# Agent attention with two feed-forward layers: an earlier query load, a second order for the last steps, shared PSUM tiles in the first block, and GpSimd rounding in 23 steps

## The chip, the core and the metric

The kernel runs on one core of a Trainium2 chip. The metric is device time in microseconds (us). The kernel before takes 1104.78 us (median of 3 runs, 1104.61 to 1104.95).

## The reference

For 12480 tokens of width 128 and 49 agents, with a softmax over the last axis of scaled products:

```python
agent_v = softmax(scale * agents @ k.T) @ v
x       = softmax(scale * q @ agents.T) @ agent_v
h  = x @ moe_w_in                                  # 128 -> 2048
g  = where(h >= 1, h, where(h <= -1, 0, (h + 1)**2 / 4))
y  = g @ moe_w_out                                 # 2048 -> 128
h2 = y @ moe2_w_in
out = (s * relu(h2)**2 + b) @ moe2_w_out
```

## The kernel before, in words

Products are made from operands split into a rounded high part and a low rest (type fp32r): high·high, high·low and low·high are added in PSUM.

**Prologue** (`agents_values`, up to about 68 us): key scores, softmax over tokens, `agent_v`, decoding of the weights, and the product of `agent_v` with the first layer's weights, left in `awh` and `awl` by `weights_high` (L500) and `weights_low` (L504).

**Blocks and steps.** The tokens stand in 25 blocks: the first 256 wide, then 23 of 512, the last 448. A block has 8 steps in each layer (`JP`), and a step makes two chunks of 128 of the 2048 hidden features, so there are 200 steps (`NS`). A narrow step's elementwise tile is 128x512 (two chunks of 256 tokens), a wide one's 128x1024.

**One step of layer 1** is a chain over the engines: `H` on TensorE (L602, or the pair L632 and L638 from block 2 on), `R` on ScalarE (`relu`, L651), `S` on ScalarE (`square`, L657), `M` on VectorE (`cap`, L661, reads PSUM and SBUF), `g` the rounding to the high part (`hi`: L670 on ScalarE or L672 on VectorE), `L` on VectorE (`lo`, L677: two SBUF inputs, the low part), `O` on TensorE (L716, summed over the block's 8 steps in PSUM tile `y`). Layer 2 has the same letters in small (`h r s l o`; in the steady lists `t` is the square, `G` and `C` the rounding on ScalarE or VectorE), with no cap, and its sum lies in PSUM tile `o`. `Y` and `y` take the sum of layer 1 out as high and low part (L735, L738); `Z` takes the result out (L742) and issues its DMA. Layer 2 runs `D` = 11 steps behind layer 1.

**Who rounds.** `PAT1` = "10011010001001" says it for the first 14 steps of layer 1 (1 is ScalarE: steps 0, 3, 4, 6, 10, 13); all other steps of layer 1 round on VectorE. Layer 2 follows `PAT2`, three quarters on ScalarE, and its last 11 steps round on VectorE. GpSimd does nothing after the constants at the start.

**Queries.** `load_q(t)` (L160) issues block t's queries on the SP queue into one of two buffers. `q_scores` (L169) makes 4 products with the agents, and ten small operations on ScalarE and VectorE (`z` in the ramp's order: L176, L186 to L199) make the softmax. `q_transpose` (L212) turns it to `pt`; from block 2 on, SP also issues two DMAs `pt<-pt` and four `px<-pt` (L226, L228), whose rows the second half of the pair step (L638) reads.

**PSUM.** Tag `h` has three tiles of two banks, one tile per H or h, per `q_scores` and per `q_transpose`. Tags `y` and `o` have one bank each.

**Order.** Each engine works its queue in program order, and the program's order is written out. After the prologue, `fill_rows` (L607) issues eight DMAs on SP that copy `awh` and `awl` into other layouts. Then `ramp` (L749) follows the string `RAMP`, from H of step 0 to step 13. Then `steady` (L767) takes the steps two at a time: for each pair `n0` it adds the tokens of `PAIR` to a list per engine, and a loop emits from the lists while dependencies hold. In `PAIR`, layer 1's step is n0 or n0+1, the layer 2 step of `h` and `r` is m = n - 11, `t`, `G`, `C` and `l` are of step m-1, `O` is n-2 and `o` is m-2. The same lists serve the last pairs (n0 = 200 to 214), where no H is left.

Of the kernel before, what the change touches and what calls it, by code (L numbers as in the profile page):

```python
# [18 lines left out]
def kernel(  # L19
# [17 lines left out]
    nc = tc.nc  # L37
    P = 128
# [8 lines left out]
    XN = 2 * X1  # L47
    XL = NA - XN

    GR, XB, UB, WB, KV = 4, 3, 4, 2, 7  # L50
    WARM, CD = 10, 1
    PAT1, PAT2, TL = "10011010001001", "11011101", 11

# [22 lines left out]
        "v11 v12 D1 q1"  # L76
    )
    RAMP = (
# [5 lines left out]
    )  # L84
    WORD = "A0 A2 A1 B0 B1 C0 C1 D0 D1".split()
    PIECE = {"A0": (0, 512), "A2": (512, 512)}
# [2 lines left out]
        "PE": "H0 h0 O0 o0 q0 O1 p1 p0 h1 q1 o1".split(),  # L89
        "ACT": "t0 P0 Y0 R0 R1 Q0 S0 S1 G0 r0 P1 Y1 t1 r1 Q1 G1".split(),  # L90
        "DVE": "L0 y0 C0 C1 Z1 F0 M0 M1 l0 Z0 c0 y1 c1 L1 l1 F1".split(),
    }
    QS, QT, DX = 7, 5, 1
    MASK_H = 0x7FFFFE00
# [64 lines left out]
        q_t[t] = qp.tile([P, TB], F32, tag="q", name=f"q{t}")  # L159
        nc.sync.dma_start(out=q_t[t][:, :w], in_=qT[:, t0:t0 + w])  # L160

    def q_scores(t):
        if t >= NB:
            return []
        qt = q_t.pop(t)
        sc = ps_h(f"qs{t}")
        scv = sc[:, 0, 0:4 * NA].rearrange("p (c a) -> p c a", a=NA)
        for i, c0 in enumerate(subs(t)):
            nc.tensor.matmul(out=scv[:, i, :], lhsT=qt[:, c0:c0 + P], rhs=aT, start=True, stop=True)  # L169
        e = small.tile([P, 4, NA], F32, tag="qe", name=f"qe{t}")  # L170
        mx = small.tile([P, 4], F32, tag="qm", name=f"qm{t}")
        sm = small.tile([P, 4], F32, tag="qsm", name=f"qsm{t}")
        pt = ptok[t % NPT]
        parts = [(P, 0, len(subs(t)))]
        ops = [
            lambda n=n, a=a, b=b: nc.scalar.activation(out=e[:n, a:b, :], in_=scv[:n, a:b, :], func=ACTF.Copy)  # L176
            for n, a, b in parts
        ]
        qev.extend(ops)
        ops = []  # L180
        for n, a, b in parts:
            ev, mv, sv = e[:n, a:b, :], mx[:n, a:b], sm[:n, a:b]
            wide = [n, b - a, NA]
            ph, pl = pt[:n, a:b, 0:NA], pt[:n, a:b, LO:LO + NA]
            ops += [
                lambda ev=ev, mv=mv: nc.vector.tensor_reduce(out=mv, in_=ev, op=ALU.max, axis=AX.X),  # L186
                lambda ev=ev, mv=mv, wide=wide: nc.vector.tensor_tensor(
                    out=ev, in0=ev, in1=mv.unsqueeze(2).to_broadcast(wide), op=ALU.subtract
                ),
                lambda ev=ev: nc.scalar.activation(out=ev, in_=ev, func=ACTF.Exp, scale=scale),  # L190
                lambda: None,
                lambda ev=ev, sv=sv: nc.vector.tensor_reduce(out=sv, in_=ev, op=ALU.add, axis=AX.X),
                lambda sv=sv: nc.vector.tensor_scalar_add(sv, sv, 1e-9),
                lambda sv=sv: nc.vector.reciprocal(out=sv, in_=sv),
                lambda ev=ev, sv=sv, wide=wide: nc.vector.tensor_tensor(
                    out=ev, in0=ev, in1=sv.unsqueeze(2).to_broadcast(wide), op=ALU.mult
                ),
                lambda ev=ev, ph=ph: nc.vector.tensor_copy(out=ph, in_=ev),
                lambda ev=ev, ph=ph, pl=pl: nc.vector.tensor_tensor(  # L199
                    out=pl, in0=ev, in1=ph.bitcast(F32), op=ALU.subtract  # L200
                ),
            ]
        return ops

    def q_transpose(t):
        if t >= NB:
            return
        fill(len(fillers))
        w = blocks[t][1]
        tp = ps_h(f"tp{t}")[:, 0, :]  # L210
        for i, c0 in enumerate(subs(t)):
            nc.tensor.matmul(  # L212
                out=tp[:, c0:c0 + P], lhsT=ptok[t % NPT][:, i, :], rhs=ident_r,
                start=True, stop=True,
            )
        pt = pt_t[t] = ptp.tile([P, TB], F32R, tag="pt", name=f"pt{t}")
        if t >= QB:
            px = px_t[t] = late.tile([P, TB], F32R, tag="px", name=f"px{t}", bufs=2)

        def spread():  # L220
            nc.scalar.activation(out=pt[:, :w], in_=tp[:, :w], func=ACTF.Copy)
            if t < QB:
                return
            src = pt.bitcast(F32)
            for i, r in enumerate((NA, LO + NA)):
                nc.sync.dma_start(out=src[r:r + X1, :w], in_=src[i * X1:(i + 1) * X1, :w])  # L226
            for g in range(P // RG):
                nc.sync.dma_start(out=px.bitcast(F32)[g * RG:g * RG + XL, :w], in_=src[XN:NA, :w])  # L228

        qev.append(spread)  # L230
# [353 lines left out]
    D1, D2 = 2, 2  # L584
    D = JP + D1 + DX
    hp, gx, gh, gl = {}, {}, {}, {}
    y_ps, y_hl, o_ps = {}, {}, {}

    def H(layer, n):
        t, j = divmod(n, JP)  # L590
        w = blocks[t][1]
        h = ps_h(f"h{layer}_{n}")
        for i in range(2):
            sl = slice((2 * j + i) * P, (2 * j + i + 1) * P)
            if layer == 1:
                rhs = pt_t[t][:, :w]
                ops = [(awh, rhs), (awl, rhs)]
            else:
                yh, yl = y_hl[t]
                ops = [(wi2h, yh[:, :w]), (wi2h, yl[:, :w]), (wi2l, yh[:, :w])]  # L600
            for m, (a, r) in enumerate(ops):
                nc.tensor.matmul(  # L602
                    out=h[:, i, :w], lhsT=a[:, sl], rhs=r, start=(m == 0), stop=(m == len(ops) - 1)
                )
        hp[layer, n] = h
# [54 lines left out]
        x, h = gv(gx, 1, n), gv(hp, 1, n)  # L660
        nc.vector.scalar_tensor_tensor(out=x, in0=h, scalar=1.0, in1=x, op0=ALU.max, op1=ALU.min)  # L661

    def hi(layer, n, on_act):
        kind = GH(layer, n)
        if (kind == "1") != on_act:
            return
        gh[layer, n] = ring("gh", layer, n, F32R, GR)
        x, a = gv(gx, layer, n), gv(gh, layer, n)
        if on_act:
            nc.scalar.activation(out=a, in_=x, func=ACTF.Copy)  # L670
        else:
            nc.vector.tensor_copy(out=a, in_=x)  # L672

    def lo(layer, n):
        gl[layer, n] = ring("gl", layer, n, F32R, GR)
# [7 lines left out]

    def GH(layer, n):
        if layer == 1:
            return PAT1[n] if n < len(PAT1) else "0"
        return PAT2[n % len(PAT2)] if n < NS - TL else "0"

    def last_step(first):
# [59 lines left out]
    def ramp():  # L749
        steps = {}  # L750

        def first_q(k):
            ops = q_scores(k)
            steps[k] = [q_evac, *ops[:3], *ops[4:]]

        does = {
            "H": lambda n: H(1, n), "R": lambda n: relu(1, n), "S": lambda n: square(1, n), "M": cap,
            "g": lambda n: hi(1, n, GH(1, n) == "1"), "L": lambda n: lo(1, n), "O": lambda n: O(1, n),
            "h": lambda n: H(2, n), "r": lambda n: relu(2, n), "s": lambda n: square(2, n),
            "G": lambda n: hi(2, n, GH(2, n) == "1"), "l": lambda n: lo(2, n), "o": lambda n: O(2, n),  # L760
            "Y": lambda: evac(1, "h"), "y": lambda: evac(1, "l"),
            "u": load_q, "q": first_q, "p": q_transpose, "P": lambda n: q_evac(), "z": lambda k, i: steps[k][i](),
        }
        for token in RAMP.split():
            does[token[0]](*[int(x) for x in token[1:].split(".") if x])

    def steady():  # L767

        lists = {e: [] for e in PAIR}

        def first(n):
            t, j = divmod(n, JP)
# [15 lines left out]
            fillers.extend(later.pop(0))  # L788

        for n0 in range(NR, NS + D + D2 + 2, 2):  # L790
            for e, tokens in PAIR.items():
                for token in tokens:
                    c, n = token[0], n0 + int(token[1])
                    m, j, t = n - D, n % JP, n // JP
# [5 lines left out]
                        return [slots[-4]] if len(slots) > 3 else []  # L800

                    def add(key, deps, fn, *args):
                        lists[e].append((key, deps, fn, args))

                    if c == "H" and a and n == n0:
                        add(("H", n), slot(("M", n)) + slot(("M", n + 1)), first, n)
# [20 lines left out]
                    elif c == "M" and a:  # L827
                        add(("M", n), [("S", n)], cap, n)
                    elif c == "c" and a:
                        add(("c", n), [("M", n), ("O", n - GR)], hi, 1, n, False)  # L830
                    elif c == "L" and n - 1 < NS:
                        add(("L", n - 1), [("c", n - 1), ("O", n - 1 - GR)], lo, 1, n - 1)
                    elif c == "r" and 0 <= m < NS - 1:
# [3 lines left out]
                    elif c == "t" and 0 <= m - 1 < NS - 1:  # L837
                        add(("t", m - 1), [("r", m - 1)], square, 2, m - 1)
                    elif c in "GC" and 0 <= m - 1 < NS - 1 and (c == "G") == (GH(2, m - 1) == "1"):
                        add(("g", m - 1), [("t", m - 1), ("o", m - 1 - GR)], hi, 2, m - 1, c == "G")  # L840
                    elif c == "l" and 0 <= m - 1 < NS - 1:
                        add(("l", m - 1), [("g", m - 1), ("o", m - 1 - GR)], lo, 2, m - 1)
                    elif c == "l" and m - 1 == NS - 1:
# [20 lines left out]
    with tc.manual_schedule():  # L864
        prologue()
        late = ctx.enter_context(tc.tile_pool(name="late", bufs=1))
        fill_rows()
        ramp()
        fillers.append(lambda: nc.vector.tensor_scalar_mul(bcol, bcol, b_sb[:, 0:1]))
# [36 lines left out]
```

## Time and profile before

| | us |
|---|---|
| runs, median of 3 | 1104.78 |
| the profiled execution | 1106.68 |
| its span, first to last instruction | 1104.9 |
| busy in the span: TensorE, ScalarE, VectorE | 1072.0, 969.9, 964.8 |
| busy GpSimd, all in the first 2 us | 0.8 |

The profiled execution is 1.90 us (0.17%) above the median, and 1.78 us of it lie outside the span. Busy times are shares of one execution; TensorE's are modelled, since matmuls overlap. An entry like `[5.12 <-DMA q<-in_qT]` behind an instruction says that its engine was idle that long before it and what ended the idle time. `x2` means that the row holds two consecutive instructions.

### The profile page before, as it was taken

To read this page: it belongs to the slowest core of one execution; us is meant where nothing else is said; L and a number is where in the kernel's file an instruction comes from. 1 tells how busy PE (TensorE), PEld (TensorE's weight loads), DVE (VectorE), ACT (ScalarE), POOL (GpSimd) and SP (SyncE) were. 2 spreads that over 40 slices of the span, in tenths; PEclk is the share of its full clock that TensorE was granted. 3 is DMA by queue.
4 is the path that set the end of the run, shared out by engine and by line. 5 is a ranking of instruction groups with operands and counts; after the bars stand their busy time and mean duration, and the time that the engine had idled before them with its cause. 6 is when DMAs were issued, how large, how long until landed. Compare 5 with 4: busy or idle time off the path is not lost.

```text
span 1104.9 us, 13492 instructions
## 1 busy us (share of the span) xinstructions
PE 1072.0 (97%) x5050; PEld 823.4 (75%) x5050; DVE 964.8 (87%) x1194; ACT 969.9 (88%) x1132; POOL 0.8 (0%) x7
## 2 busy tenths in 40 slices
PE   6887999999999999999999999999999999999997
PEld 2676777777777777777777777777777777777776
DVE  8887889889889889889889889889889889889875
ACT  6876899889889889889889989989989989989974
POOL 0000000000000000000000000000000000000000
PEclk9898999999999999999999999999999999999999
DMA  9920000000000000000000000000000000000000
GB/s 351 394 79 23 19 23 24 4 28 24 4 28 25 3 28 25 3 27 26 3 27 26 3 27 26 2 27 27 1 28 27 1 27 27 1 18 18 1 10 18
DMA packets 19973, 41.01 MB, mean 37 GB/s; under 512 B 2638, under 2 KB 7976, under 8 KB 19268
## 3 DMA queue, kind: packets, MB, share of 16 engines
q1 hardware_dynamic: 19908, 40.15, 10.6%
q8 instruction: 40, 0.66, 0.3%
q14 instruction: 25, 0.20, 0.1%
HBM read 27.58 MB, written 6.39 MB: 31 GB/s over the span
## 4 chain that ended last, share of the span: by engine, by line
PE 89%; DVE 5%; ACT 2%; DMA 1%; SPq 1%; issue 1%; DVEq 0%
PE h L602 26%; PE o L716 24%; PE y L716 23%; PE h L632 7%; PE h L638 4%; PE qs L169 2%; DVE gl L677 1%; DMA k<-in_kT 1%; DVE x L661 1%; PE tp L212 1%; PE av L457 1%; ACT x L657 1%; SPq L616 1%; DVE gh L672 1%; DVE mxs L414 1%
## 5 line engine op out<-in xcount | busy, mean ns | idle before, releaser
L677 DVE TENSOR_TENSOR gl<-x,gh 128x1024 fp32r<-128x1024 f32 (+2 forms) x399 | 469.4, 1193 | 20.0 <-ACT gh L670 19.8
L657 ACT ACTIVATE x<-x 128x1024 f32<-128x1024 f32 (+2 forms) x399 | 404.4, 1043 | 1.9
L661 DVE SCALAR_TENSOR_TENSOR x<-h,x 128x1024 f32<-128x1024 f32 (+2 forms) x200 | 230.5, 1192 | 77.0 <-ACT x L657 76.4
L653 ACT ACTIVATE x<-h 128x1024 f32<-128x1024 f32 (+2 forms) x199 | 201.3, 1012 | 59.6 <-PE h L602 59.6
L651 ACT ACTIVATE x<-h 128x1024 f32<-128x1024 f32 (+2 forms) x200 | 190.0, 1005 | 2.9 <-DVE gl L677 1.0
L672 DVE CAST gh<-x 128x1024 fp32r<-128x1024 f32 (+2 forms) x251 | 164.0, 678 | 15.4 <-ACT x L657 15.2
L602 PE MATMUL h<-yh,wi2h 128*128 128x512 f32 (+2 forms) x400 | 166.7, 417 | 0.9 <-DVE x L661 0.9
L716 PE MATMUL o<-gl,wo2h 128*128 128x512 f32 (+2 forms) x400 | 157.9, 395 | 5.2 <-DVE gl L677 5.2
L716 PE MATMUL o<-gh,wo2h 128*128 128x512 f32 (+2 forms) x400 | 157.7, 394 | 1.9 <-DVE osb L742 1.8
L716 PE MATMUL y<-gl,wo1h 128*128 128x512 f32 (+2 forms) x400 | 156.6, 391 | 1.3 <-DVE gl L677 1.3
L716 PE MATMUL y<-gh,wo1h 128*128 128x512 f32 (+2 forms) x400 | 156.2, 391 | 0.1
L716 PE MATMUL y<-gh,wo1l 128*128 128x512 f32 (+2 forms) x400 | 156.2, 390 | 0.0
L716 PE MATMUL o<-gh,wo2l 128*128 128x512 f32 (+2 forms) x400 | 155.6, 389 | 0.0
L602 PE MATMUL h<-yh,wi2l 128*128 128x512 f32 (+2 forms) x400 | 155.5, 389 | 0.0
L602 PE MATMUL h<-yl,wi2h 128*128 128x512 f32 (+2 forms) x400 | 155.4, 389 | 0.0
L670 ACT ACTIVATE gh<-x 128x1024 fp32r<-128x1024 f32 (+1 forms) x148 | 152.2, 1030 | 0.9 <-DVE x L661 0.8
L602 PEld LDWEIGHTS h<-yh,wi2h 128*128 128x128 f32 x400 | 75.0, 187 | 36.7 <-issue 17.0
L632 PE MATMUL h<-pt,awm 128*128 128x512 f32 (+1 forms) x368 | 99.2, 391 | 0.0
L716 PEld LDWEIGHTS o<-gl,wo2h 128*128 128x128 f32 x400 | 75.0, 188 | 28.3 <-DVE gl L677 12.2
L716 PEld LDWEIGHTS y<-gl,wo1h 128*128 128x128 f32 x400 | 75.6, 189 | 19.7 <-DVE gl L677 2.8
L716 PEld LDWEIGHTS o<-gh,wo2h 128*128 128x128 f32 x400 | 75.2, 188 | 18.8 <-DVE osb L742 2.1
L716 PEld LDWEIGHTS y<-gh,wo1h 128*128 128x128 f32 x400 | 75.6, 189 | 17.3 <-ACT gh L670 0.3
(114 smaller groups left out, 909.8 us busy)
## 6 DMA issues: line engine op xcount, KB each, us to landing
k<-in_kT SPq DMA_DIRECT2D x12, 512.0 KB, 12.7
v<-in_v_main SPq DMA_DIRECT2D x12, 512.0 KB, 8.5
q<-in_qT SPq DMA_DIRECT2D x23, 256.0 KB, 4.9
out_T<-osb SPq DMA_DIRECT2D x23, 256.0 KB, 2.1
wu<-in_w_in SPq DMA_DIRECT2D x4, 1024.0 KB
px<-pt SPq DMA_DIRECT2D x88, 38.0 KB
wu<-in_w_out SPq DMA_DIRECT2D x3, 1024.0 KB
pt<-pt SPq DMA_DIRECT2D x44, 30.0 KB
```

Source lines behind the costliest of these rows:

```text
L169: nc.tensor.matmul(out=scv[:, i, :], lhsT=qt[:, c0:c0 + P], rhs=aT, start=True, stop=True)
L602: nc.tensor.matmul(out=h[:, i, :w], lhsT=a[:, sl], rhs=r, start=(m == 0), stop=(m == len(ops) - 1))
L632: nc.tensor.matmul(out=out[g], lhsT=awm[:, c * P:(c + 1) * P], rhs=pt_t[t][:, :w], start=True, stop=False)
L638: nc.tensor.matmul(out=out[g], lhsT=awx[r, q], rhs=px_t[t][r, :w], start=False, stop=True)
L651: nc.scalar.activation(out=x, in_=h, func=ACTF.Relu, scale=0.5, bias=0.5)
L653: nc.scalar.activation(out=x, in_=h, func=ACTF.Relu)
L657: nc.scalar.activation(out=x, in_=x, func=ACTF.Square)
L661: nc.vector.scalar_tensor_tensor(out=x, in0=h, scalar=1.0, in1=x, op0=ALU.max, op1=ALU.min)
L670: nc.scalar.activation(out=a, in_=x, func=ACTF.Copy)
L672: nc.vector.tensor_copy(out=a, in_=x)
L677: nc.vector.tensor_tensor(out=b, in0=x, in1=a.bitcast(F32), op=ALU.subtract)
L716: nc.tensor.matmul(out=o[:, :w], lhsT=l[:, c, :], rhs=r[:, i, :w], start=(c == 0 and m == 0), stop=(c == KF - 1 and m == 2),)
```

## The change

Four edits and a new order.

1. `load_q(2)` is called ahead of `fill_rows`; before it stood first in `RAMP`, behind the copies on SP.
2. In the ramp, the scores of blocks 1 and 2 and the transpose of block 1 take PSUM tile `o` in place of an `h` tile. The first block's 8 steps are 256 wide, and two steps now share one `h` tile, each with one bank.
3. The rounding `g` of layer 1 runs on GpSimd (`tensor_copy`) in steps 0 to 22 (`NP`); `PAT1` is gone. In `steady`, these go to a list of their own (POOL).
4. From n0 = 200 on, the lists follow `TAIL`. On TensorE the first `O` comes ahead of `h`; on VectorE each rounding `C` is followed at once by its own `l`, with `L0` behind `l0` and `Z0` ahead of `C1`.
5. `RAMP` is a new order of the same work.

```diff
-    PAT1, PAT2, TL = "10011010001001", "11011101", 11
+    PAT2, TL, NP = "11011101", 11, 23
...
     RAMP = (
-        "u2 H0 q1 R0 H1 S0 z1.0 M0 R1 z1.1 H2 g0 z1.2 H3 z1.3 L0 S1 z1.4 O0 R2 M1 R3 z1.5 H4 g1 z1.6 S2 L1 S3 z1.7 "
-        "O1 M2 R4 z1.8 H5 g2 S4 z1.9 L2 R5 M3 S5 O2 M4 g3 p1 M5 H6 g4 L3 P1 H7 L4 R6 O3 g5 R7 O4 L5 S6 H8 S7 M6 O5 "
-        "M7 g6 q2 u3 R8 g7 L6 H9 L7 z2.0 S8 z2.1 O6 z2.2 R9 M8 O7 Y z2.3 H10 g8 S9 y H11 L8 R10 M9 O8 R11 z2.4 S10 "
-        "g9 h0 z2.5 L9 S11 M10 r0 O9 s0 z2.6 M11 g10 H12 G0 z2.7 h1 L10 R12 H13 g11 r1 O10 z2.8 S12 L11 s1 l0 O11 "
-        "R13 z2.9 M12 G1 o0 S13 l1 h2 g12 p2 r2 M13 P2 L12 g13"
+        "H0 q1 R0 H1 S0 H2 z1.0 M0 H3 R1 z1.1 H4 g0 R2 z1.2 H5 z1.3 S1 L0 z1.4 S2 O0 M1 R3 z1.5 H6 M2 g1 S3 H7 z1.6 "
+        "z1.7 g2 L1 z1.8 O1 R4 L2 S4 M3 O2 R5 z1.9 g3 M4 p1 S5 g4 L3 P1 M5 O3 R6 L4 g5 S6 H8 R7 M6 O4 S7 L5 g6 q2 u3 "
+        "M7 R8 L6 O5 g7 z2.0 O6 S8 z2.1 L7 H9 z2.2 M8 z2.3 O7 R9 H10 z2.4 g8 z2.5 Y z2.6 S9 z2.7 H11 y z2.8 L8 R10 "
+        "S10 M9 O8 R11 M10 g9 h0 S11 z2.9 H12 g10 L9 r0 s0 M11 O9 R12 L10 g11 G0 h1 S12 H13 l0 L11 r1 O10 R13 M12 O11 "
+        "s1 S13 g12 h2 G1 M13 o0 r2 p2 L12 g13 P2 l1"
     )
...
+    TAIL = {
+        "PE": "H0 O0 h0 o0 O1 h1 o1".split(),
+        "ACT": "Y0 R0 S0 t0 G0 r0 Y1 R1 S1 t1 G1 r1 P0 P1 Q0 Q1".split(),
+        "DVE": "C0 l0 L0 M0 y0 Z0 c0 F0 C1 l1 L1 M1 y1 Z1 c1 F1".split(),
+    }
...
-    def q_scores(t):
+    def q_scores(t, early=False):
...
-        sc = ps_h(f"qs{t}")
-        scv = sc[:, 0, 0:4 * NA].rearrange("p (c a) -> p c a", a=NA)
+        sc = ps_o(f"qs{t}") if early else ps_h(f"qs{t}")[:, 0, :]
+        scv = sc[:, 0:4 * NA].rearrange("p (c a) -> p c a", a=NA)
...
-        tp = ps_h(f"tp{t}")[:, 0, :]
+        tp = ps_o(f"tp{t}") if early else ps_h(f"tp{t}")[:, 0, :]
...
     def H(layer, n):
         t, j = divmod(n, JP)
         w = blocks[t][1]
-        h = ps_h(f"h{layer}_{n}")
+        if layer == 1 and n < JP:
+            if n % 2 == 0:
+                pairs.append(ps_h(f"h{layer}_{n}"))
+            h = pairs[-1][:, n % 2, :].rearrange("p (i w) -> p i w", i=2)
+        else:
+            h = ps_h(f"h{layer}_{n}")
...
-    def hi(layer, n, on_act):
-        kind = GH(layer, n)
-        if (kind == "1") != on_act:
-            return
+    def hi(layer, n):
...
-        if on_act:
+        kind = GH(layer, n)
+        if kind == "1":
             nc.scalar.activation(out=a, in_=x, func=ACTF.Copy)
         else:
-            nc.vector.tensor_copy(out=a, in_=x)
+            (nc.gpsimd if kind == "P" else nc.vector).tensor_copy(out=a, in_=x)
...
         if layer == 1:
-            return PAT1[n] if n < len(PAT1) else "0"
+            return "P" if n < NP else "0"
...
-        lists = {e: [] for e in PAIR}
+        lists = {e: [] for e in (*PAIR, "POOL")}
...
-            for e, tokens in PAIR.items():
+            for e, tokens in (PAIR if n0 < NS else TAIL).items():
...
-                        lists[e].append((key, deps, fn, args))
+                        lists["POOL" if key[0] == "c" and n < NP else e].append((key, deps, fn, args))
...
         late = ctx.enter_context(tc.tile_pool(name="late", bufs=1))
+        load_q(2)
         fill_rows()
         ramp()
```

## Rows read from the trace of the kernel before

**Rows 1.** Busy times by stretch: length, PE, PEld, DVE, ACT, POOL, PEclk, DMA share, GB/s.

```profile
68.56:83.32 14.76, 13.20 (x86) 10.91 (x84) 13.11 (x27) 13.06 (x26) 0.00 (x0) 1.00 0.33 77
83.32:88.44 5.12, 0.00 (x0) 0.03 (x1) 1.63 (x3) 0.95 (x2) 0.00 (x0) 1.00 0.37 116
88.44:95.30 6.86, 6.86 (x27) 6.28 (x28) 2.87 (x5) 2.94 (x6) 0.00 (x0) 0.51 0.01 2
95.30:110.00 14.70, 13.92 (x72) 11.20 (x71) 14.70 (x22) 13.73 (x19) 0.00 (x0) 1.00 0.00 0
68.56:150.00 81.44, 71.58 (x383) 57.37 (x382) 68.03 (x103) 65.90 (x96) 0.00 (x0) 0.96 0.11 31
150.00:1050.00 900.00, 899.91 (x4106) 693.63 (x4105) 807.44 (x957) 821.09 (x918) 0.00 (x0) 1.00 0.06 18
...
1097.05:1104.90 7.85, 4.01 (x19) 3.16 (x17) 3.27 (x6) 2.13 (x4) 0.00 (x0) 1.00 0.08 29
```

**Rows 2.** Timeline of TensorE around the wait for block 2's queries.

```profile
88.44 1.78 PE L169 MATMUL qs<-a,q 128*128 128x49 f32 x8 [5.12 <-DMA q<-in_qT]
```

**Rows 3.** Timeline of the SP queue, 54 to 85 us: start, length, engine, line, operation.

```profile
54.64 0.43 SPq L385 DMA_DIRECT2D b_sb<-in_b  x1
69.66 0.90 SPq L613 DMA_DIRECT2D awm<-awh  x1
...
82.34 2.07 SPq L160 DMA_DIRECT2D q<-in_qT  x2
```

**Rows 4.** TensorE's waits, 1060 to 1105 us: who for whom, us, times, longest.

```profile
PE o L716 <- DVE gl L677: 4.2, 4, 1.6
PE o L716 <- DVE osb L742: 1.8, 1, 1.8
```

**Rows 5.** Timeline of VectorE, last steps.

```profile
1061.15 2.23 DVE L677 TENSOR_TENSOR gl<-x,gh 128x1024 fp32r<-128x1024 f32 x2 [0.93 <-ACT gh L670]
...
1093.25 0.63 DVE L672 CAST gh<-x 128x896 fp32r<-128x896 f32 x1 [2.78 <-ACT x L657]
1093.79 2.09 DVE L677 TENSOR_TENSOR gl<-x,gh 128x896 fp32r<-128x896 f32 x2
```

**Rows 6.** VectorE by line and form, 68.56 to 150 us: count, busy, mean ns, idle before.

```profile
L672 DVE CAST gh<-x 128x1024 fp32r<-128x1024 f32 x13 | 8.7, 688 | 0.0
L672 DVE CAST gh<-x 128x512 fp32r<-128x512 f32 x6 | 2.5, 424 | 0.1
```

**Rows 7.** ScalarE by line and form, same stretch.

```profile
L670 ACT ACTIVATE gh<-x 128x512 fp32r<-128x512 f32 x10 | 6.2, 626 | 0.2 <-DVE x L661 0.2
L670 ACT ACTIVATE gh<-x 128x1024 fp32r<-128x1024 f32 x4 | 4.2, 1058 | 0.6 <-DVE x L661 0.6
```

**Rows 8.** GpSimd by line and form, all it does (three of seven).

```profile
masks.py:199 POOL TENSOR_SCALAR_AFFINE_SELECT ident<-ident 128x128 f32<-128x128 f32 x1 | 0.3, 292 | 0.1
masks.py:197 POOL MEMSET ident<- 128x128 f32 x1 | 0.2, 204 | 0.3 <-POOLq L896 0.3
...
L896 POOL MEMSET const-float32-0.0<- 128x1 f32 x1 | 0.1, 103 | 0.2 <-issue 0.2
```

**Rows 9.** Timeline of TensorE, block 2's transpose and first use of its rows.

```profile
108.03 0.56 PE L212 MATMUL tp<-ident_r,ptok 128*128 128x128 f32 x4
...
120.00 0.50 PE L638 MATMUL h<-px,awx 19*128 19x512 f32 x1 [0.49 <-DMA px<-pt]
```

**Rows 10.** Timeline of ScalarE, last steps.

```profile
1062.10 1.06 ACT L670 ACTIVATE gh<-x 128x1024 fp32r<-128x1024 f32 x1
...
1092.26 0.95 ACT L657 ACTIVATE x<-x 128x896 f32<-128x896 f32 x1
```

**Rows 11.** Timeline of TensorE, last steps: step 199's `O`, and two neighbours of step 195's `o`.

```profile
1064.77 0.36 PE L716 MATMUL y<-gl,wo1h 128*128 128x448 f32 x1
...
1085.98 0.36 PE L716 MATMUL o<-gh,wo2l 128*128 128x448 f32 x1
1086.18 0.36 PE L716 MATMUL o<-gl,wo2h 128*128 128x448 f32 x1
```

More of the change, by code (lines that the diff above doesn't have):

```diff
@@ L203, in q_scores, with q_transpose @@
         return ops
-    def q_transpose(t):
+    def q_transpose(t, early=False):
         if t >= NB:
@@ L586 @@
     hp, gx, gh, gl = {}, {}, {}, {}
+    pairs = []
     y_ps, y_hl, o_ps = {}, {}, {}
@@ L752, in first_q @@
         def first_q(k):
-            ops = q_scores(k)
+            ops = q_scores(k, True)
             steps[k] = [q_evac, *ops[:3], *ops[4:]]
@@ L757, in ramp @@
             "H": lambda n: H(1, n), "R": lambda n: relu(1, n), "S": lambda n: square(1, n), "M": cap,
-            "g": lambda n: hi(1, n, GH(1, n) == "1"), "L": lambda n: lo(1, n), "O": lambda n: O(1, n),
+            "g": lambda n: hi(1, n), "L": lambda n: lo(1, n), "O": lambda n: O(1, n),
             "h": lambda n: H(2, n), "r": lambda n: relu(2, n), "s": lambda n: square(2, n),
-            "G": lambda n: hi(2, n, GH(2, n) == "1"), "l": lambda n: lo(2, n), "o": lambda n: O(2, n),
+            "G": lambda n: hi(2, n), "l": lambda n: lo(2, n), "o": lambda n: O(2, n),
             "Y": lambda: evac(1, "h"), "y": lambda: evac(1, "l"),
-            "u": load_q, "q": first_q, "p": q_transpose, "P": lambda n: q_evac(), "z": lambda k, i: steps[k][i](),
+            "u": load_q, "q": first_q, "p": lambda k: q_transpose(k, k == 1), "P": lambda n: q_evac(),
+            "z": lambda k, i: steps[k][i](),
         }
@@ L829, in steady @@
                     elif c == "c" and a:
-                        add(("c", n), [("M", n), ("O", n - GR)], hi, 1, n, False)
+                        add(("c", n), [("M", n), ("O", n - GR)], hi, 1, n)
                     elif c == "L" and n - 1 < NS:
@@ L839, in steady @@
                     elif c in "GC" and 0 <= m - 1 < NS - 1 and (c == "G") == (GH(2, m - 1) == "1"):
-                        add(("g", m - 1), [("t", m - 1), ("o", m - 1 - GR)], hi, 2, m - 1, c == "G")
+                        add(("g", m - 1), [("t", m - 1), ("o", m - 1 - GR)], hi, 2, m - 1)
                     elif c == "l" and 0 <= m - 1 < NS - 1:
```

## The prediction

> **What bounds the kernel now.** I read the table by stretch first, to see where time can be had at all. From 150 to 1050 us TensorE is busy 899.91 of 900 us [rows 1]: there it is the bound, no edit takes work off it, and I cost the edits there at nothing (a shorter load on VectorE or ScalarE hides under TensorE). That leaves the ramp, 68.56 to 150 us, and the last steps, 1067 to 1097 us. The ramp lasts 81.44 us with TensorE, VectorE and ScalarE busy 71.58, 68.03 and 65.90: three engines near each other, none full. The reader should see two things in its parts. From 83.32 to 88.44 TensorE does nothing, and from 88.44 to 95.30 it runs at a granted clock of 0.51, the lower level of 1.2 GHz; before and after it is 1.00. And from 95.30 to 110 VectorE is busy 14.70 of 14.70 us: after the stall it is the bound.
>
> Next, the timeline, for what ended the empty stretch: block 2's queries, 5.12 us [rows 2]. Their DMA stands on SP behind the eight copies, which SP works off from 69.66 on; it is issued at 82.34, as the first of two [rows 3]. The SP queue has nothing to do from 55.07 (54.64 + 0.43) to 69.66.
>
> Last, TensorE's waits near the end: five, of 6.0 us together, four on a layer 2 subtraction and one on `Z` [rows 4]. The reason is in the order: VectorE must do `C` of step m ahead of `l` of step m-1, and `C` waits, 2.78 us in the row shown, for a square that follows `h` of step m [rows 5].
>
> **The earlier query load.** SP is free at 55.07 and the buffer is that of block 0, whose scores lie in the prologue. So the load starts some 27 us earlier and lands long before the scores want it. It stays off SP's copies, which are held by `awh` until 69.66 anyway; the 2.07 us for two query loads [rows 3] fall in a gap. The price is nothing, the 5.12 us go, and with no idle stretch in front I expect no half clock behind. What this returns I take from VectorE's account, since it is the next bound: its idle time in the two stretches is 5.12 - 1.63 + 6.86 - 2.87 = 7.48 us [rows 1].
>
> **Rounding on GpSimd.** Of the 23 roundings, VectorE loses 4 narrow and 13 wide (8, 9, 11, 12 and 14 to 22), ScalarE 4 narrow and 2 wide. VectorE: 4 x 0.424 + 13 x 0.688 = 10.64 us [rows 6]. ScalarE: 4 x 0.626 + 2 x 1.058 = 4.6 us [rows 7].
>
> The price of one on GpSimd is not in the trace; it has only small operations there [rows 8]. The memset grows by (204 - 103)/127 = 0.80 ns a column, the select, which also reads SBUF, by (292 - 103)/127 = 1.49 ns. For a wide tile of 1024 columns that gives 0.1 + 0.8 = 0.9 us and 0.1 + 1.5 = 1.6 us; eight selects whole would be 2.3 us. I take 1.2 us for a wide one and 0.65 us for a narrow one, between memset and select, since a copy reads like the one and computes as little as the other. The Trainium skill, GPSIMD Engine Reference, section 4.1, says one-input operations there run roughly at line rate; by that a wide one is estimated at some 0.9 us.
>
> All 23 would be 8 x 0.65 + 15 x 1.2 = 23.2 us, spread over some 60 us, so GpSimd is no bound by itself. What counts is whether a rounding holds VectorE up, by coming later than `L` wants it, or by slowing VectorE's own work while both run. No row shows the two engines working at once. The ends are 0 and 23.2 us. I take half, 11.6 us: VectorE's order puts one `M` between most roundings and their `L` (M10 z2.9 L9, M11 L10), which covers about half of each. The Trainium skill, SBUF — State Buffer, section "Who interferes with whom", speaks against this edit: a VectorE instruction with two SBUF inputs and a GpSimd instruction that reads SBUF exclude each other for a whole instruction. By it the hold-up would be nearer 23 us; no run here shows that yet.
>
> **The sum of the ramp.** VectorE's 81.44 us are 68.03 busy and 13.41 idle, of which 7.48 is named above and 5.93 lies elsewhere. After: 68.03 - 10.64 + 11.6 + 5.93 = 74.9 us, a gain of 6.5 us. With no hold-up it would be 63.3, but TensorE cannot follow: its 71.58 busy us, with the 6.86 at half clock halved, are 68.2, and it will not lose every other wait. One that stays is block 2's rows: from its transpose at 108.03 to their arrival at 120.00 pass 12 us of DMA [rows 9], and TensorE was already 0.49 us early for them. A faster ramp waits here next, by some 2 us. So the upper end is 81.44 - 68.2 - 2 = 11 us. With the full 23.2 it would be 86.5, a loss of 5.1 us.
>
> **PSUM tiles.** The scores and the transpose leave tag `h`, and the first 8 steps take 4 tiles rather than 8, so TensorE can run up to 6 steps ahead. `o` is unused until layer 2's first `o`, behind all three in the queue. In that stretch VectorE is busy 13.11 of 14.76 us [rows 1], so slots decide little: between 0 and 1.65 us, VectorE's idle time there; I take 0. The new ramp order moves no work between engines, and I give it no term of its own; it spends ScalarE's 4.6 us to stay clear of VectorE.
>
> **The last steps.** With `C` followed by its own `l`, the work for `o` of step m-1 no longer waits for step m. After `h` come `r` and `t` at some 0.95 us each [rows 10], `C` with 0.63 and `l` with 2.09/2 = 1.05 us [rows 5], 3.6 us. TensorE has four groups of six matmuls in between, at a spacing of 1086.18 - 1085.98 = 0.20 us [rows 11] 4.8 us: the waits go. Each is worth its idle time and the 0.16 us by which a matmul's record (0.36) outlasts its spacing: 6.0 + 5 x 0.16 = 6.8 us. The cost is new: `L` of step 199 now stands behind `l` of 188, which waits for ScalarE's rounding, 1062.10 to 1063.16 [rows 10]. In the old order it was the second of the pair at 1061.15 [rows 5]; now it ends at 1063.2 + 1.2 + 1.05 = 1065.45 (1.2 for the wide subtraction, 2.23 less 1.05 [rows 5]), and the matmul that read it at 1064.77 [rows 11] waits 0.7 us. Behind that on ScalarE stand `Y` and then the square of step 189, which move by the same 0.7; `l` of 189 still comes before TensorE gets to it. The gain is 6.8 - 0.7 = 6.1 us; 4 to 6.8 as ends, 4 if one or two waits return at `Z`, whose slack is only about 0.4 us. The final 7.85 us from 1097.05 on [rows 1] are unchanged.
>
> **Total.** 6.5 + 6.1 = 12.6 us. The profiled execution took 1106.68 us with a span of 1104.9; the median is 1.90 us lower. I subtract from the median: 1104.78 - 12.6 = 1092.2 us.
>
> **Rivals.** (1) GpSimd holds nobody up: ramp 11, tail 6.1, so 1104.78 - 17.1 = 1087.7 us. For: VectorE has 5.9 us of slack and the order leaves an `M` between. Against: 46 subtractions in these steps compete with 23 roundings.
>
> (2) Every rounding is a full hold-up, as when no subtraction can run beside a rounding: ramp -5.1, tail +6.1, so 1103.8 us, no change that can be measured. Against: half of `L`'s neighbours are `M`, which reads one operand from PSUM. This rival is the rule that the Trainium skill states in SBUF — State Buffer, taken to its end.
>
> (3) Slower: GpSimd's price. If a wide rounding costs eight selects, 2.3 us, a narrow one 1.17, and both hold VectorE throughout, its work is 68.03 - 10.64 + 8 x 1.17 + 15 x 2.3 + 5.93 = 107.2 us, 25.7 more than before; less 6.1 it is 1124 us. It turns into a loss where the hold-ups reach 81.44 + 6.1 - 63.3 = 24.2 us, 1.27 us for a wide one (19 wide equivalents). Against: eight starts are counted where there is one.
>
> (4) The last steps keep their waits, for a dependency that I missed: ramp 6.5 alone, 1098.3 us.
>
> **How the numbers follow.** Forecast 0.57, rival 1 0.21, rival 4 0.09, rival 2 0.08, rival 3 0.05. About 0.2% (2.2 us) is what a measurement of this kernel can tell from no change. Faster: 0.57 + 0.21 + 0.09 and a little of rival 2, 0.90; same 0.06; slower 0.04. The range takes in rival 1 and rival 4 and the forecast's own ends: 1086 to 1099 us.
>
> **What would show it.** Right: no empty stretch near 83 us, a granted clock of 1.00 from 70 us on, block 2's load on SP near 55 us, VectorE without `C` between `l` rows at the end, and TensorE's waits there under 1 us. GpSimd's rounding near 1.2 us, and subtractions that keep the 1.2 us of a wide one [rows 5], or come out longer where a rounding runs beside them. A new wait on `px` of about 2 us would be right too. Wrong: roundings of 2 us or more; TensorE idle in the ramp waiting for `gl` behind GpSimd; a half clock that returns; a stall of `h` of step 192 on `yl`, which VectorE now makes after `l` of 189.

## The result and the profile after

The changed kernel takes 1092.59 us (median of 4 runs, 1092.12 to 1094.44) against 1104.87 us before: a ratio of 0.9888, 95% interval 0.9871 to 0.9906. The forecast was 1092.2 us, in a range of 1086 to 1099.

The table by stretch of the changed kernel, with the columns of [rows 1] (length, PE, PEld, DVE, ACT, POOL, PEclk, DMA share, GB/s). The fourth row is the ramp up to the place that stands at 150 us in the trace of before; the last is the stretch in which TensorE waited five times before.

```profile
55.00:68.05 13.05, 11.22 (x109) 8.23 (x108) 11.26 (x19) 9.72 (x20) 0.00 (x0) 1.00 0.33 120
68.05:83.32 15.27, 12.72 (x93) 11.41 (x92) 12.56 (x24) 11.27 (x21) 5.29 (x7) 1.00 0.33 75
83.32:95.30 11.98, 9.88 (x49) 7.04 (x48) 11.71 (x18) 10.18 (x14) 4.07 (x4) 1.00 0.10 29
...
68.05:141.78 73.73, 67.74 (x383) 54.39 (x382) 65.75 (x87) 62.33 (x89) 24.59 (x22) 1.00 0.12 30
141.78:1042.80 901.02, 900.92 (x4110) 694.59 (x4108) 807.64 (x957) 822.41 (x919) 1.05 (x1) 1.00 0.06 18
...
1059.00:1082.40 23.40, 23.40 (x112) 20.73 (x111) 17.46 (x21) 18.20 (x20) 0.00 (x0) 1.00 0.03 12
```

The reader sees three things: the granted clock is 1.00 in all of them; the empty stretch is gone; and TensorE is busy 23.40 of 23.40 us near the end, where it was 23.86 of 29.84 in the kernel before:

```profile
1067.21:1097.05 29.84, 23.86 (x108) 19.69 (x107) 18.35 (x23) 17.22 (x19) 0.00 (x0) 1.00 0.03 9
```

The SP queue, against [rows 3], shows why the empty stretch is gone: block 2's queries are issued at 55.83, ahead of the copies.

```profile
55.01 0.78 SPq L392 DMA_DIRECT2D b_sb<-in_b  x1
55.83 0.54 SPq L167 DMA_DIRECT2D q<-in_qT  x1
69.15 0.90 SPq L626 DMA_DIRECT2D awm<-awh  x1
```

TensorE's timeline keeps two waits that the prediction named: the rows `px` of block 2 (1.06 us, answering to [rows 9]), and `O` of step 199 (0.54 us), the only one left in the last steps, where [rows 4] had five.

```profile
101.93 0.56 PE L219 MATMUL tp<-ident_r,ptok 128*128 128x128 f32 x4
...
113.79 0.49 PE L651 MATMUL h<-px,awx 19*128 19x512 f32 x1 [1.06 <-DMA px<-pt]
...
1057.37 0.47 PE L727 MATMUL y<-gl,wo1h 128*128 128x448 f32 x1 [0.54 <-DVE gl L688]
```

**A measure for the rest.** Whole times scatter by one to two microseconds, and the profiled executions begin the first H anywhere from 66.93 to 68.88 us, also where the program up to there is the same. So traces are compared from the first H on, by the start of three groups of TensorE instructions: the first H, the pair of steps 24 and 25, and the last pair of layer 1 (steps 198 and 199). In the changed kernel these are the rows

```profile
68.29 0.29 PE L615 MATMUL h<-pt,awh 128*128 128x256 f32 x1
...
149.15 1.08 PE L645 MATMUL h<-pt,awm 128*128 128x512 f32 x4
...
1042.80 0.98 PE L645 MATMUL h<-pt,awm 128*128 128x448 f32 x4
```

and in the kernel before they start at 68.80, 157.37 and 1050.91. This gives the table below for all kernels of this study whose ends are compared; a missing record can shift an entry by 0.2 us. Each row is one execution, and its whole time can lie off the median: those of e4, e9, e10, e13 and e14 were the slowest of their four, those of e1 and e5 the fastest. "First H to 24" is the ramp, "198 to end" the last steps.

| kernel | us, median | first H at | first H to 24 | 24 to 198 | 198 to end |
|---|---|---|---|---|---|
| before | 1104.87 | 68.80 | 88.57 | 893.54 | 53.99 |
| changed | 1092.59 | 68.29 | 80.86 | 893.65 | 47.50 |
| e1 queries alone | 1098.49 | 67.07 | 80.83 | 893.35 | 53.95 |
| e2 last steps alone | 1098.16 | 66.99 | 88.63 | 893.38 | 47.50 |
| e3 changed, no GpSimd | 1095.08 | 67.22 | 85.32 | 893.32 | 47.54 |
| e4 changed, old tiles | 1094.30 | 67.82 | 83.30 | 893.47 | 47.51 |
| e5 changed, queries late | 1099.71 | 66.93 | 88.40 | 893.37 | 47.50 |
| e9 changed, 200 steps | 1090.92 | 67.94 | 82.33 | 891.93 | 47.50 |
| e10 changed, px first, L first | 1091.43 | 67.92 | 83.50 | 893.31 | 46.77 |
| e12 queries and last steps | 1091.09 | 67.56 | 80.83 | 893.53 | 47.58 |
| e13 e12, GpSimd 14 to 22, L first | 1089.07 | 68.88 | 80.01 | 893.56 | 46.75 |
| e14 e13 with the tiles | 1089.63 | 68.11 | 80.54 | 893.56 | 46.69 |

The ramp gained 88.57 - 80.86 = 7.7 us, the last steps 53.99 - 47.50 = 6.5, the 893 us between nothing. By the traces that is 14.1 us from the first H on; by the medians it is 12.3. The profiled execution of before was 1.8 us above the median of 1104.87, and its first H came at 68.80, where e2, e7 and e8, the same program up to there, have 66.99, 67.37 and 67.61; that this is the cause is argued, not shown. The changed kernel also gives back 0.5 us outside the span: time less span is 2.24 to 2.32 us in all four runs of the changed kernel, and 2.2 to 2.3 in e4, e5 and e10, against 1.78 in the profiled run of before and 1.7 to 1.8 in all other kernels of the table. Why is open.

### The profile page after: what moved, and what is told of

The parts are those of the page before. It is cut to its first block, busy times and chain, and to the rows that moved or that the text cites. A ratio compares the mean times of both kernels' runs of the same rounds, so it can differ in the third digit from the quotient of the medians.

```text
span 1090.3 us, 13529 instructions
## 1 busy us (share of the span) xinstructions
PE 1065.9 (98%) x5050; PEld 819.7 (75%) x5050; DVE 962.9 (88%) x1177; ACT 967.1 (89%) x1126; POOL 26.5 (2%) x30
## 4 chain that ended last, share of the span: by engine, by line
PE 90%; DVE 5%; ACT 2%; DMA 2%; issue 1%; SPq 1%; POOL 0%; DVEq 0%; POOLq 0%; ACTq 0%
PE h L615 26%; PE o L727 25%; PE y L727 23%; PE h L645 8%; PE h L651 4%; PE qs L176 2%; DMA k<-in_kT 1%; DVE x L674 1%; DVE gl L688 1%; PE tp L219 1%; PE av L464 1%; DMA px<-pt 1%; DVE mxs L421 1%; ACT x L664 1%; ACT x L670 1%
## 5 line engine op out<-in xcount | busy, mean ns | idle before, releaser
L688 DVE TENSOR_TENSOR gl<-x,gh 128x1024 fp32r<-128x1024 f32 (+2 forms) x399 | 474.2, 1205 | 22.5 <-ACT gh L681 21.6
L683 DVE CAST gh<-x 128x1024 fp32r<-128x1024 f32 (+2 forms) x234 | 153.6, 680 | 6.7 <-ACT x L670 6.7
L681 ACT ACTIVATE gh<-x 128x1024 fp32r<-128x1024 f32 (+1 forms) x142 | 147.8, 1041 | 0.0
L727 PEld LDWEIGHTS y<-gh,wo1l 128*128 128x128 f32 x400 | 75.1, 188 | 17.0
```

Source lines behind the costliest of these rows:

```text
L683: (nc.gpsimd if kind == "P" else nc.vector).tensor_copy(out=a, in_=x)
L688: nc.vector.tensor_tensor(out=b, in0=x, in1=a.bitcast(F32), op=ALU.subtract)
L727: nc.tensor.matmul(out=o[:, :w], lhsT=l[:, c, :], rhs=r[:, i, :w], start=(c == 0 and m == 0), stop=(c == KF - 1 and m == 2),)
```

## The experiments

**e1: the query load alone.** The kernel before with

```diff
-        "u2 H0 q1 R0 H1 S0 z1.0 M0 R1 ...
+        "H0 q1 R0 H1 S0 z1.0 M0 R1 ...
...
+        load_q(2)
         fill_rows()
```

> The kernel before with the earlier query load alone. Theory: it is worth the empty stretch of 5.12 us and part of the half clock behind it; VectorE, busy 13.1 of 14.8 us ahead and 14.7 of 14.7 behind, takes over as the bound, and its idle time in the two stretches, 7.5 us, is what comes back: 5 to 7.5 us faster, 1097.3 to 1099.8, and no granted clock under 1.00 between 70 and 150 us. Rival: the wait goes to the next thing that is late (PSUM tiles, or the rows px), and under 3 us are left of it.

Measured: 1098.49 us, ratio 0.9944 (0.9927 to 0.9961), so 6.2 us faster by the ratio. The stretch from 67 to 150 us, columns as above, shows no lower clock and VectorE at 75.34 of 83.00 us:

```profile
67.00:150.00 83.00, 78.28 (x428) 61.83 (x428) 75.34 (x113) 72.70 (x103) 0.00 (x0) 1.00 0.12 32
```

From the first H to step 24 it takes 80.83 us, 7.7 less than before, and within 0.1 of the changed kernel. So the wait went and nothing took its place, as the theory had it: 6.2 us lie in its 5 to 7.5, 7.7 a little above. That VectorE's idle time sets the size is less sure: TensorE's own account, the 5.12 us and half of the 6.86 at half clock, gives 8.5, and the run does not tell the two apart. And there is more in it than was expected: this one edit already does all that the whole change does to the ramp.

**e2: the order of the last steps alone.** The kernel before with `TAIL` for n0 >= `NS` in the loop of `steady`.

> The kernel before with the own order of the last steps alone. Theory: five waits of TensorE go, one of about 0.7 us comes at L of step 199, so 5.9 to 6.5 us faster, 1098.3 to 1098.9; from the last pair of layer 1 products (1050.91 in the trace of before, 53.99 us ahead of the end) to the end about 47.5 us. Rival: part of the gain in the last steps came from what runs ahead of them, and the order alone gives under 4 us.

Measured: 1098.16 us, ratio 0.9938 (0.9924 to 0.9953), so 6.9 us faster, a little more than the theory's 5.9 to 6.5. From the last pair to the end 47.50 us, which the theory had as 47.5, and the same as in the changed kernel. The two edits do not touch each other.

**e5: the queries late again.** The changed kernel with `load_q(2)` behind `fill_rows()`.

> The changed kernel with the load of block 2's queries back behind the eight copies on SP, all else as changed. Theory: the stall returns, and with it the lower clock: TensorE waits for q some 5 to 6 us from about 82 us on, a stretch at a granted clock near 0.5 follows, and the time is 5 to 7.5 us above the changed kernel's, 1097.6 to 1100. Rival: with more slack ahead (GpSimd's relief, tiles, new order) the wait hides in part and costs under 3 us.

Measured: 1099.71 us, ratio 0.9953 (0.9938 to 0.9969), and 88.40 us from first H to step 24, 7.5 more than in the changed kernel. TensorE's timeline, and the stretch behind it:

```profile
86.69 1.92 PE L176 MATMUL qs<-a,q 128*128 128x49 f32 x8 [5.99 <-DMA q<-in_qT]
```

```profile
85.50:92.40 6.90, 5.71 (x24) 5.45 (x25) 3.35 (x6) 1.65 (x3) 0.87 (x1) 0.53 0.02 7
```

An idle stretch of 5.99 us ends in a granted clock of 0.53, the lower of the two levels, 1.2 GHz. Put in or taken out, alone or with all the rest, the query load is worth 7.5 to 7.7 us by the traces; by the times it is 6.2 (e1) and 7.1 (e5).

**e3: no GpSimd.** The changed kernel with the old `PAT1` for the first 14 steps and VectorE for the others.

> The changed kernel, ramp order and all, with the roundings of layer 1 back on ScalarE and VectorE as in the kernel before. Theory: GpSimd takes 10.6 us off VectorE and gives some 6 us back as longer subtractions, so without it the ramp is 2 to 4 us longer: 1094.6 to 1096.6. Rival 1: the hold-ups eat all of it, and the time is within 1 us of 1092.6. Rival 2: the new ramp order is made for GpSimd's delay and loses more than 5 us without it.

Measured: 1095.08 us, ratio 0.9907 (0.9892 to 0.9922), 2.5 us above the changed kernel by the medians. But its ramp is 4.5 us longer, and two stretches of it ran at a lower clock, with no long idle time of TensorE in front:

```profile
75.70:79.20 3.50, 2.97 (x14) 2.97 (x15) 3.27 (x7) 2.90 (x6) 0.00 (x0) 0.58 0.17 54
...
113.20:120.10 6.90, 5.88 (x19) 4.87 (x20) 4.38 (x6) 5.20 (x7) 0.00 (x0) 0.54 0.02 7
```

The number fits the theory, but the trace doesn't show its cause; part of the 4.5 us is the clock. This run does not settle what GpSimd is worth. e12 says what it is worth together with the tiles and the new order.

**e4: the old PSUM tiles.** The changed kernel with `ps_h` for the scores and the transpose, and a tile to each step.

> The changed kernel with PSUM as before: each of the first 8 steps, the scores and the transpose again take an h tile of their own. Theory: the tiles let TensorE run ahead, but VectorE and ScalarE set the pace there, so 0 to 1.6 us slower, 1092.6 to 1094.2. Rival: the new order puts six H in front of the first O and needs the tiles; TensorE waits for M of earlier steps and the ramp loses 3 us or more.

Measured: 1094.30 us, ratio 0.9897 (0.9882 to 0.9912), 1.7 us above the changed kernel by the medians, 2.4 by the ramp. TensorE now waits 2.5 us for `M` in the ramp, in three waits, where the changed kernel had 0.2 in one; and a stretch at a lower clock follows here too:

```profile
PE h L615 <- DVE x L674: 2.5, 3, 1.8
```

```profile
73.80:80.70 6.90, 6.36 (x30) 5.96 (x29) 5.55 (x12) 2.66 (x5) 2.90 (x5) 0.52 0.30 86
```

The longest of the three waits, 1.80 us, stands right before the lower clock. So the rival's mechanism is there, between theory and rival in size, but how much of the 2.4 us is the wait and how much the clock stays open. That the new order needs the tiles is not shown: the four runs of e4 (1091.86 to 1094.41 us) and of the changed kernel (1092.12 to 1094.44) overlap, and so do the intervals of their ratios.

**e7 and e8: GpSimd beside VectorE.** The kernel before, with GpSimd work added in steps 40 to 79, where TensorE is the bound; the output is not touched.

```diff
+            if layer == 1 and 40 <= n < 80:
+                nc.gpsimd.tensor_copy(out=scr, in_=a.bitcast(F32))          # e7
...
+                nc.gpsimd.tensor_copy(out=scr[:, 0:2], in_=a[...][:, 0, 0:2])  # e8
+                nc.gpsimd.memset(scr, 0.0)
```

> The kernel before with one more GpSimd copy of the wide high part to a scratch tile in each of steps 40 to 79, where TensorE is the bound; output unchanged. Theory: a GpSimd copy that reads SBUF and a VectorE instruction with two SBUF inputs exclude each other, while M, which reads one operand from PSUM, runs on: in these steps the wide subtraction's mean goes from 1.22 us to 1.35 us or more, M stays at 1.22, the copy takes 1.05 us alone and 1.5 us or more in the mean. Rival: both share bandwidth, and then M and the subtraction both get longer, by a few per cent each.

> The same, but GpSimd fills the scratch tile with zeros (after a copy of two columns that paces it) rather than copying: it writes as much and reads almost nothing. Theory: what excludes is the reading; the subtraction's mean stays within 0.03 us of 1.22 us. VectorE's rounding, one SBUF input, may still get longer where it runs beside the fill. Rival: writing excludes as well, and the subtraction gets longer as with the copy.

Measured: 1122.96 us with the copy, 1108.67 with the fill, against 1105.30 before (one run each). Groups by line and form from 330 to 520 us (count, busy us, mean ns, idle before), the kernel before:

```profile
L677 DVE TENSOR_TENSOR gl<-x,gh 128x1024 fp32r<-128x1024 f32 x76 | 91.4, 1220 | 3.4 <-ACT gh L670 3.4
L661 DVE SCALAR_TENSOR_TENSOR x<-h,x 128x1024 f32<-128x1024 f32 x36 | 42.4, 1219 | 13.2 <-ACT x L657 13.2
L672 DVE CAST gh<-x 128x1024 fp32r<-128x1024 f32 x47 | 31.1, 688 | 0.0
```

e7:

```profile
L682 DVE TENSOR_TENSOR gl<-x,gh 128x1024 fp32r<-128x1024 f32 x69 | 96.0, 1413 | 0.8 <-ACT gh L671 0.8
L662 DVE SCALAR_TENSOR_TENSOR x<-h,x 128x1024 f32<-128x1024 f32 x36 | 42.4, 1219 | 14.2 <-ACT x L658 14.2
L673 DVE CAST gh<-x 128x1024 fp32r<-128x1024 f32 x43 | 29.6, 711 | 0.0
...
L677 POOL COPY scr<-gh 128x1024 f32<-128x1024 f32 x24 | 48.5, 2019 | 85.7 <-DVE gh L673 85.1
```

and e8:

```profile
L683 DVE TENSOR_TENSOR gl<-x,gh 128x1024 fp32r<-128x1024 f32 x74 | 89.0, 1218 | 3.2 <-ACT gh L671 3.2
L662 DVE SCALAR_TENSOR_TENSOR x<-h,x 128x1024 f32<-128x1024 f32 x37 | 43.6, 1219 | 13.2 <-ACT x L658 13.2
L673 DVE CAST gh<-x 128x1024 fp32r<-128x1024 f32 x47 | 32.5, 716 | 0.0
...
L678 POOL MEMSET scr<- 128x1024 f32 x24 | 23.4, 975 | 1.4
```

A GpSimd copy that reads SBUF lengthens the subtraction, which has two SBUF inputs, from 1.22 to 1.41 us in the mean, and is itself 2.02 us long; `M`, which has one, stays at 1.22. A fill leaves the subtraction alone; VectorE's own rounding gets a little longer beside either, 0.69 to 0.71 and 0.72 us. That is the theory, and not the rival of a shared bandwidth, by which `M` would be longer too. The ramp of the changed kernel shows the exclusion singly. GpSimd's rounding runs from 86.78 to 87.83, and a VectorE operation on 4 columns that takes 0.16 us when nothing is beside it ends with it; a pair of roundings takes 2.18 us and 1.91 us is a single one. That small operation has one SBUF input, as `M` has; so one SBUF input alone does not spare an operation:

```profile
86.78 1.05 POOL L683 CAST gh<-x 128x1024 fp32r<-128x1024 f32 x1 [2.29 <-DVE x L674]
91.36 2.18 POOL L683 CAST gh<-x 128x1024 fp32r<-128x1024 f32 x2 [3.54 <-DVE x L674]
95.89 1.91 POOL L683 CAST gh<-x 128x1024 fp32r<-128x1024 f32 x1 [2.34 <-DVE x L674]
```

```profile
73.90 0.16 DVE L200 TENSOR_SCALAR qsm<-qsm 128x4 f32<-128x4 f32 x1
...
86.92 0.93 DVE L200 TENSOR_SCALAR qsm<-qsm 128x4 f32<-128x4 f32 x1
...
92.55 2.07 DVE L688 TENSOR_TENSOR gl<-x,gh 128x1024 fp32r<-128x1024 f32 x1
```

This agrees with the Trainium skill, SBUF — State Buffer, "Who interferes with whom": whichever of the two starts first has the shared pair of ports for its whole length. The unhindered price of a wide rounding is the 1.05 us of the first row.

**e9: GpSimd in all 200 steps.** The changed kernel with `NP` = 200.

> The changed kernel with the roundings of layer 1 on GpSimd in all 200 steps rather than 23. Theory: from 150 us on TensorE is the bound and VectorE has 10 per cent of slack, so longer subtractions cost nothing there: within 1.5 us of 1092.6. VectorE's wide subtraction keeps a mean near 1.4 us throughout. Rival: GpSimd's rounding comes late for L, or holds VectorE up so that O waits in every pair: 10 us or more slower.

Measured: 1090.92 us, ratio 0.9872 (0.9854 to 0.9890), a little beyond the theory's 1.5 us, on the faster side. The wide subtraction's mean from 145 to 1040 us is 1346 ns, and yet:

```profile
145.00:1040.00 895.00, 895.00 (x4092) 691.90 (x4091) 748.79 (x780) 817.37 (x914) 258.25 (x176) 1.00 0.06 18
```

VectorE is busy 749 of 895 us where the changed kernel has 808 of 901: the roundings that left it weigh more than the longer subtractions. From step 24 to 198 it is even 1.7 us shorter, though TensorE is the bound there. The trace shows where: in the changed kernel the weight load in front of one `o` per block waits 0.2 us for a subtraction, 21 times from 152 to 1030 us, and in e9 never; one pair of steps per block takes 9.95 us rather than 10.03. Its ramp is 1.5 us longer, with 3.5 us of it at a clock of 0.56.

**e10: two further edits.** The changed kernel with the `px` copies issued ahead of the `pt` copies in `spread`, and `L0` ahead of `C0 l0` in `TAIL`.

> The changed kernel with two further edits: the four px copies are issued ahead of the two pt copies, and in the first pair of the last steps L of step 199 comes ahead of l of step 188. Theory: the wait of 1.06 us on px and the one of 0.54 us on gl at the end go, each with 0.16 us around it: 1.5 to 2 us faster than the changed kernel, 1090.6 to 1091.1; tail from the last pair of layer 1 products to the end 46.8 us rather than 47.5. Rival: the pt copies, now 2.5 us later, hold the first half of the pair step up instead, or o of step 188 waits for its l, and nothing is gained.

Measured: 1091.43 us, ratio 0.9882 (0.9866 to 0.9898). That is 0.3 us above the theory's 1090.6 to 1091.1. The last steps take 46.77 us, 0.73 less, as the theory had it, and no wait of TensorE is left there. The first edit fell to its rival:

```profile
112.04 2.07 PE L645 MATMUL h<-pt,awm 128*128 128x512 f32 x4 [1.54 <-DMA pt<-pt]
```

The wait moved from `px` to `pt` and grew from 1.06 to 1.54 us; 6.9 us at a clock of 0.52 follow it, so the 2.6 us that the ramp is longer are not the wait alone.

**e12, e13, e14: which edits carry the gain.** e12 is the kernel before with the query load and `TAIL`. e13 adds GpSimd in steps 14 to 22, behind the written order, and `L0` ahead; e14 adds the tiles to that.

```diff
-            return "P" if n < NP else "0"
+            return PAT1[n] if n < len(PAT1) else "P" if n < NP else "0"   # e13, with the old RAMP
```

> The kernel before with the earlier query load and the own order of the last steps, and nothing else: old ramp order, old PSUM tiles, no rounding on GpSimd. Theory: these two are the whole gain, since the query load alone brought the last pair of layer 1 products 7.9 us nearer to the first H, and the changed kernel 7.6: from first H to last pair 974.2 us, tail 47.5, the same time as the changed kernel within 1 us, 1091.6 to 1093.6. Rival: GpSimd, tiles and the new order are worth 2.5 us as the kernel without GpSimd suggests: 1094.5 or more.

> As the last, and GpSimd rounds in steps 14 to 22 alone, where the written order does not apply; L of step 199 comes ahead of l of step 188. Theory: the old order reaches block 2's transpose 2.1 us sooner than the new one (31.5 us after the first H against 33.6), GpSimd takes 2 us off the stretch behind it (47.2 against 49.3) of which the wait on px keeps one, and the tail is 46.8: 1.5 to 2.5 us faster than the changed kernel, 1090 to 1091. Rival: the gain behind the transpose belongs to the new order, and only the 0.7 us of the tail is left.

> As the last, with the changed kernel's PSUM tiles (two steps to a tile in the first block; scores and first transpose in o). Theory: the old order, which runs H at most three steps ahead, has no use for them: within 0.6 us of the last, by first H to last pair. Rival: the tiles are worth their 2.4 us in the old order too.

Measured: e12 1091.09 us, ratio 0.9874 (0.9859 to 0.9889); e13 1089.07 us, ratio 0.9854 (0.9837 to 0.9870); e14 1089.63 us, ratio 0.9862 (0.9847 to 0.9877). e12 equals the changed kernel in every stretch of the table: 80.83 against 80.86 and 47.58 against 47.50. So the two edits are the whole gain, and GpSimd in the ramp, the tiles and the new order together are worth nothing. By the medians e12 is 1.5 us faster, just beyond its theory; 0.5 of that lies outside the span, and the intervals overlap. The same ramp repeats well when no lower clock falls into it by chance: before and e2 have 88.57 and 88.63, e1 and e12 both 80.83.

That nothing has two sides. TensorE's rows for block 2's transpose, in e1 and in e13, both in the old order:

```profile
98.57 0.56 PE L212 MATMUL tp<-ident_r,ptok 128*128 128x128 f32 x4
```

```profile
100.42 0.56 PE L219 MATMUL tp<-ident_r,ptok 128*128 128x128 f32 x4
```

In e1 it stands 98.57 - 67.07 = 31.5 us behind the first H; in the changed kernel 101.93 - 68.29 = 33.6. From there to step 24, e1 takes 147.90 - 98.57 = 49.3 us, the changed kernel 47.2. The new order with GpSimd loses 2.1 us ahead of the transpose and wins 2.1 back behind it. e13 keeps the whole of the first and less than half of the second: 100.42 - 68.88 = 31.5 us ahead of the transpose, and 148.89 - 100.42 = 48.5 behind it, 0.9 less than e12's 49.4. So of the 2.1 us behind the transpose GpSimd in steps 14 to 22 brings 0.9, not the theory's 2; the tiles are not the rest, since e14 has them and takes the same 48.5 there. That leaves the new order, with GpSimd in the steps ahead of 14; the two were not separated. The ramp takes 80.01 us, 0.8 less than in the changed kernel, and the tail 0.75 less. From the first H to the end it takes 1089.2 - 68.88 = 1020.3 us against 1090.3 - 68.29 = 1022.0, 1.7 less and in the theory's 1.5 to 2.5; by the medians it is 3.5. Its interval ends at 0.9870, where that of the changed kernel begins at 0.9871: it has the lowest median of all, but its interval overlaps those of e9, e10, e12 and e14. e14's tiles do not help the old order (80.54 against 80.01; 3.5 us of its ramp ran at a clock of 0.56).

## Why the prediction was right

**The earlier load.** Priced at nothing, with 7.48 us of VectorE's idle time coming back: measured 7.7 (e1) and 7.5 (e5). No half clock behind it: right for the changed kernel.

**GpSimd.** The sum had 10.64 us off VectorE and 11.6 us of hold-ups, a net loss of 1.0 us, the tiles and the order at 0. Measured for the three together: 80.86 against 80.83, so 0.0. The two terms were less good. VectorE's groups of the changed kernel from 68.05 to 141.78 us:

```profile
L688 DVE TENSOR_TENSOR gl<-x,gh 128x1024 fp32r<-128x1024 f32 x16 | 22.5, 1412 | 0.7 <-ACT gh L681 0.6
L688 DVE TENSOR_TENSOR gl<-x,gh 128x512 fp32r<-128x512 f32 x16 | 12.6, 788 | 0.0
L202 DVE TENSOR_TENSOR qe<-qe,qsm 128x196 f32<-128x196 f32 x3 | 1.5, 499 | 0.1
L200 DVE TENSOR_SCALAR qsm<-qsm 128x4 f32<-128x4 f32 x3 | 1.3, 420 | 0.1
```

Before, the same forms took 1219, 686, 357 and 165 ns. The excess is 16 x 0.193 + 16 x 0.102 + 3 x 0.142 + 3 x 0.255 = 5.9 us, half of the 11.6; a wide rounding of 1.05 us alone was priced at 1.2, and the mean of all 15 is 1.30. In return VectorE is idle for 73.73 - 65.75 = 8.0 us, where 5.93 was kept; 4.2 of them are waits for ScalarE's squares. So the hold-up missed by 5.7 us and the idle time by 2.1, in opposite directions. The 10.64 us off VectorE came short as well: with 5.9 us back, its busy time should have fallen by 4.7 us and fell by 68.03 - 65.75 = 2.3. Some of this is that a record reaches into its follower ([rows 5]: 0.09 us at a rounding), so that 17 records taken off overstate the time; the rest was not traced. The ramp's sum came near because these misses nearly cancel, which is luck. One sign of being wrong came in part: TensorE waits 3.3 us for `gl` in the ramp, in seven waits, against 2.4 in seven in e1. VectorE itself was never idle for GpSimd.

**The wait that comes next.** "Some 2 us" on `px`: 1.06 us.

**The last steps.** 6.8 us of waits gone, 0.7 us new, 6.1 in sum: measured 6.5 (before to changed, and e2), and the new wait at step 199 was 0.54 idle and 0.16 behind it, 0.7. The waits on `gl` went as reckoned; nothing stalled at `yl` of step 192.

**The total.** The ramp's 6.5 was 7.7 and the tail's 6.1 was 6.5, 1.5 us more by the traces; against the medians' 12.3 the 12.6 looks better than its parts were, by the 1.8 us between the two measures that the result section leaves in part open.

**The rivals.** Free GpSimd (1087.7) and eight selects (1124) are both out: alone it costs 1.05 us, and it does exclude. The full hold-up (1103.8) is out too: the rule holds, but VectorE lost 5.9 us and not 23. The likely reason, read from the order and not tested, is that a rounding that starts beside `M` is over, or half over, when the subtraction comes. The last steps that keep their waits (1098.3) are out by e2.

## What to carry to other kernels

A load that an early consumer needs must not stand in a queue behind transfers that wait for late producers; it costs the idle time and the clock behind it. In an order by hand, put each conversion right in front of its own follower, since a second conversion put in between may wait on work that the follower could have hidden. Moving work to a third engine pays only where what it slows down is less than what it takes off: with the tiles and the new order it brought nothing in this ramp, alone in steps 14 to 22 some 0.9 us, and in the steps behind 1.7.

## What was not expected of the hardware

The lower clock also came without a long idle stretch of TensorE. e3, e4, e9, e10 and e14 each had a stretch of 3.5 to 6.9 us at 0.52 to 0.58 in the ramp, behind stretches in which TensorE was merely less busy: its longest wait shortly ahead was 0.6 us in e3's first, 0.7 in its second, 1.8 in e4, 1.05 in e9, 1.5 in e10 and 1.2 in e14. The changed kernel, with a wait of 1.06 us on `px`, kept 1.00. And the same prologue ran once with it and once without: the kernel before had a clock of 0.53 from 64.50 to 68.00 us and its first H at 68.80; e2, with the same program up to there, 1.00 and its first H at 66.99:

```profile
64.50:68.00 3.50, 3.08 (x7) 2.49 (x8) 3.13 (x6) 2.25 (x3) 0.00 (x0) 0.53 0.00 0
```

```profile
64.40:67.00 2.60, 2.02 (x10) 1.31 (x9) 2.60 (x4) 1.74 (x4) 0.00 (x0) 1.00 0.00 0
```

So edits of one or two microseconds in the ramp cannot be told apart by one profile. GpSimd in all steps on top of e13 suggests itself, from e9's 1.7 us between steps 24 and 198; it was not tried.
